# Six weight preparations inside the last block of layer one, in two lanes, and the first pair's ELU values in freed weight tiles

## Chip, core, metric

One core of one Trainium2 chip runs the whole program in one launch. The metric is the device time in microseconds (us), here the median of the runs shown.

## What is computed

Sliding-window attention (window 64, head size 64, 4 batches of 576 positions, 8 heads) gives a 2304 x 512 activation. Two layers follow, each with a 512 x 2048 input matrix and a 2048 x 512 output matrix:

```
x = attention(q, k, v)                      # 2304 x 512, fp32
x = square(relu(x @ moe_w_in)) @ moe_w_out  # layer one
y = elu(x @ moe2_w_in) @ moe2_w_out         # layer two
```

The weights arrive as 64-bit floats and are decoded to fp32 on the chip. Every fp32 operand is split into a high and a low part ("split": ScalarE writes the high part, VectorE the difference), and a product is three matmuls.

## The kernel before

**Layer one** takes the 2304 rows in five blocks (512, 256, 512, 512, 512), `its` in line 424. A block runs 16 iterations j, each a slice of 128 hidden columns. `m_h` (line 354) makes 12 matmuls into a PSUM tile `ph`, of which there are two; ScalarE applies Relu (line 368) and Square (line 369), and the split (line 370) makes `gs`. `m_out` (line 373) multiplies `gs` into four accumulators `o`. The loop issues `m_h` two iterations ahead of `m_out`. TensorE executes in program order, so a late Relu holds the `m_h` two iterations on, which needs its `ph` tile back.

**Layer two** computes its products by a seven-multiplication scheme on 2 x 2 blocks, over three super-blocks b of 768 rows each and eight pairs p of weight slices. `step` (line 578) is one product, six matmuls of 384 columns: numbers 1, 6, 7 and 4 accumulate in one bank `px`, and ScalarE copies `px` to `tmp` after 1, 6 and 7 (line 585); numbers 2, 5 and 3 go to `py` or `po`. `after` (line 602) adds a copy to a bank and applies `elu` (line 563: two ScalarE instructions and one VectorE instruction) into the four values `GR[p]`. The first five products of pair 0 are issued inside the last three iterations of layer one (lines 701 to 703), the rest by the list `seq` (line 721). Then `g_split` and `prod2` multiply the values with the output matrix.

**Operands of layer two** are prepared while layer one runs. `make(i, p)` (line 167) is one of 16 preparations: two loads `praw` of 512 KB, `decode64` of each (one ScalarE and four VectorE instructions), four subtractions or additions (line 184), and seven `put`s. A `put` takes a staging piece `wo` from `small`, splits into it (line 105 on ScalarE, line 106 on VectorE) and stores it to DRAM (`wd1`, `wd2`, 256 KB each). `MAKE` (line 425) names the iterations that issue a `make`; the sixteenth is issued by the `"m"` entry of `seq` at pair 1 (lines 738 and 759). After the attention's pool is closed (the list `la` is filled, line 706) `small` hands out four pieces in a ring (`gs_tile(name, HW, 4)`), and `big` the decode tiles: preparations one and three from then on use the two buffers of tag `y`, the others the old weight tiles `w0` and `w1`.

**Queues.** All transfers are issued by SyncE (SP) in one queue, in program order; an issue whose semaphores are not there yet holds those behind it. `unit_load` (line 473) loads a weight unit `wr` of layer two into a ring of eight tiles, and waits there until TensorE has finished with the ring's old content. ScalarE and VectorE also run in the order that the scheduler wrote.

Of the kernel before, what the change touches and what calls it, by code (L numbers as in the profile page):

```python
# [10 lines left out]
F32 = mybir.dt.float32  # L11
F32R = mybir.dt.float32r
# [4 lines left out]
P = 128  # L17
# [8 lines left out]
def window_attention_then_two_mlps(  # L26
# [395 lines left out]
        return ps_o.tile([P, 512], F32, tag=f"o{rot[0] % KD}", name="po")  # L422

    its = [(t, j) for t in range(NB) for j in range(NJ)]
    MAKE = {(1, 2), (1, 9)} | {(t, j) for t in (2, 3) for j in (1, 5, 9, 13)} | {(4, j) for j in (0, 1, 3, 6, 9)}
    makes = [(i, p) for i in range(2) for p in range(NP)]

    NH = 384
# [8 lines left out]
            return la[0].tile([P, 512], F32, tag="e4", name="ev", bufs=4)  # L437
        return at.tile([P, 512], F32, tag="pt", name="ev", bufs=4)

    turn = [0]  # L440

    def big(shape, name):
        if name == "y" and la:
            turn[0] += 1
        if not la or turn[0] in (1, 3):
            return wts.tile(shape, U32, tag="y", name=name, bufs=2)
        return wts.tile(shape, U32, tag="w0" if name == "y" else "w1", name=name)

    def small(shape, name):
        if la:  # L450
            return gs_tile(name, HW, 4)
        return at.tile(shape, F32R, tag="pt", name=name, bufs=4)

    g_turn = [0]
# [1 line left out]
    def gs_tile(name, n, m):  # L456
        k = g_turn[0] = (g_turn[0] + 1) % m
        if k < 4:
            return la[0].tile([P, 2, n], F32R, tag=f"gs{k}", name=name, bufs=1)
        return wts.tile([P, 2, n], F32R, tag=f"w{LA + NJ - 1}" if k == 4 else f"w{NJ - 1}", name=name)  # L460
# [114 lines left out]
    def add(out, a, b):  # L575
        nc.vector.tensor_tensor(out=out, in0=a, in1=b, op=ALU.add)  # L576

    def step(b, p, i):

        if i == 1:  # L580
            Q[b, p] = {"x": bank(2 if p % 3 == 2 else "x")}
        q = Q[b, p]
        if i in (1, 6, 7):
            prod(b, p, i, q["x"], i == 1, False)
            nc.scalar.activation(out=tmp[i], in_=q["x"][:, :NH], func=AF.Copy)  # L585
        if i == 4:
            prod(b, p, i, q["x"], False, True)
            elu(GR[p][:, 1], q["x"][:, :NH])
        if i == 2:
            q["z"] = bank("a")  # L590
            prod(b, p, i, q["z"], True, True)
        if i == 5:
            q["y"] = bank(1 if p % 2 else "a")
            prod(b, p, i, q["y"], True, False)
        if i == 3:
            prod(b, p, i, q["y"], False, True)
            g = GR[p]
            add(g[:, 2], tmp[6], q["y"][:, :NH])
            elu(g[:, 2], g[:, 2])
            add(g[:, 2], g[:, 2], g[:, 3])  # L600

    def after(b, p, i):
        q, g = Q[b, p], GR[p]
        k, n = (0, "z") if i == 2 else (3, "y")
        add(g[:, k], tmp[1 if i == 2 else 7], q[n][:, :NH])
        elu(g[:, k], g[:, k])

    SRC = {1: 0, 2: 1, 6: 0, 5: 2, 7: 0, 4: 3, 3: 1}
    XY = {}
# [1 line left out]
    def g_split(b, k, p):  # L611
        s = G[b, k, p] = gs_tile("g2", NH, 6)
        g = GR[p]
        split(s[:, 0], s[:, 1], g[:, SRC[k]], nc.vector)
        if k == 1:
            nc.vector.tensor_tensor(out=g[:, 0], in0=g[:, 2], in1=g[:, 0], op=ALU.subtract)
        if k == 2:
            nc.vector.tensor_tensor(out=g[:, 1], in0=g[:, 1], in1=g[:, 0], op=ALU.subtract)
        if k == 6:
            nc.vector.tensor_tensor(out=g[:, 0], in0=g[:, 3], in1=g[:, 0], op=ALU.subtract)  # L620

    G = {}

# [61 lines left out]
    for i, (t, j) in enumerate(its):  # L685
        if i + LA < len(its):
            m_h(*its[i + LA])
        if t + 1 < NB:
            p, r = divmod(j, 3)
            u = (t + 1, p)  # L690
            if p < HP and r == 0:
                load_to(order.index(u) + 1)
                u_S(u, a_alloc)
            elif p < HP and r == 2 and p % 2:
                u_V2([(t + 1, p - 1), u], a_alloc)
        m_out(t, j)
        if t == NB - 1 and j == NJ - 3:
            sy = [wts.tile([P, 2, NH], F32, tag="y", name="sy", bufs=2) for _ in range(2)]
            tmp.update({1: sy[0][:, 0], 6: sy[0][:, 1], 7: sy[1][:, 0]})
            tmp["r"] = [sy[1][:, 1], la[0].tile([P, NH], F32, tag="r", name="r", bufs=1)]  # L700
        if t == NB - 1 and j >= NJ - 3:
            for n in ((1, 2), (6, 5), (7,))[j - NJ + 3]:
                step(0, 0, n)
        if (t, j) == (NB - 2, 3 * HP):
            att.close()
            la.append(pool(ctx, "la", 1))
        if t == 0:
            decode(min(LA + 3 + j, NU))
        elif (t, j) in MAKE:
            make(*makes.pop(0), big, small)  # L710
        elif t == NB - 1 and j == 5:
            x_make(0)
        if t == NB - 1 and j in (8, 10, 12):
            unit_load()
    one.close()
    gb = pool(ctx, "gb", 1, side="right")
    GR += [gb.tile([P, 4, NH], F32, name=f"gr{p}") for p in range(NP)]
    for n, u in ((1, "w0"), (6, "w1"), (7, f"w{LA + NJ - 2}")):
        tmp[-n] = wts.tile([P, MT, HW], F32, tag=u, name="sk")

    seq = []
    Z = NP - 1
    for b in range(NSB):
        def S_(p, *ii, c=b):
            r = []
            for i in ii:
                r += [("s", c, p, i)] + ([("a", c, p, i)] if i in (2, 7) else [])
            return r

        def K_(k, ps=range(NP)):  # L730
            r = []
            for p in ps:
                r += [("k", b, k, p)]
            return r

        for p in range(NP):
            seq.append(("u",))
            if b == 0 and p == 1:
                seq.append(("m",))
            if p == 0:  # L740
                seq += S_(0, 6, 5, 7) if b else [("a", 0, 0, 2), ("a", 0, 0, 7)]
            else:
                seq += S_(p, 1, 2) + S_(p - 1, 3) + S_(p, 6) + S_(p - 1, 4) + S_(p, 5, 7)
        seq.append(("u",))
        seq += K_(1, (0, 1)) + S_(Z, 3, 4) + K_(1, range(2, NP)) + [("u",)] + K_(2) + [("u",)] + K_(6) + [("x", b + 1), ("u",)]
        seq += K_(5) + [("u",)] + K_(7)
        if b + 1 < NSB:
            seq += [("u",)] + S_(0, 1, 2, c=b + 1)
        seq += [("u",)] + K_(4) + [("u",)] + K_(3)
    splits = [s[1:] for s in seq if s[0] == "k"]  # L750
    AHEAD = 3
    for s in seq:
        if s[0] == "s":
            in_turn(step, *s[1:])
        elif s[0] == "a":
            after(*s[1:])
        elif s[0] == "u":
            unit_load()
        elif s[0] == "m":
            with tc.issue_after(last["act"].ins), tc.issue_after(last["dve"].ins):  # L760
                make(*makes.pop(0), big, small)
        elif s[0] == "k":
            g_split(*s[1:])
            in_turn(prod2, *s[1:])
        elif s[1] < NSB:
            x_make(s[1])
# [48 lines left out]
```

## Time and profile before

| | |
|---|---|
| median of 3 runs | 861.9 us (861.79 to 862.55) |
| the profiled execution | 858.92 us, span 857.1 us, granted clock 0.995 |
| TensorE busy (matmul / weight load) | 833.4 us (97%) / 759.2 us (89%) |
| VectorE, ScalarE busy | 598.0 us (70%), 548.3 us (64%) |
| DMA | 185.53 MB, mean 216 GB/s |

The program's last block of layer one lies at about 400 to 490 us of the span, and layer two from there to the end. In a timeline row the columns are start, duration, engine, line, operation, output and input, shape, count; the square bracket behind it is the idle time of the engine ahead of the row and what ended it. A row of a waits view gives the total, the number of waits and the longest.

### The profile page before, as it was taken

To read this page: it belongs to the slowest core of one execution; us is meant where nothing else is said; L and a number is where in the kernel's file an instruction comes from. 1 tells how busy PE (TensorE), PEld (TensorE's weight loads), DVE (VectorE), ACT (ScalarE), POOL (GpSimd) and SP (SyncE) were. 2 spreads that over 40 slices of the span, in tenths; PEclk is the share of its full clock that TensorE was granted. 3 is DMA by queue.
4 is the path that set the end of the run, shared out by engine and by line. 5 is a ranking of instruction groups with operands and counts; after the bars stand their busy time and mean duration, and the time that the engine had idled before them with its cause. 6 is when DMAs were issued, how large, how long until landed. Compare 5 with 4: busy or idle time off the path is not lost.

```text
span 857.1 us, 15143 instructions
## 1 busy us (share of the span) xinstructions
PE 833.4 (97%) x5448; PEld 759.2 (89%) x5448; DVE 598.0 (70%) x1483; ACT 548.3 (64%) x1268; POOL 5.8 (1%) x21
## 2 busy tenths in 40 slices
PE   6899999999999999999999988999999999999997
PEld 5687889998888888888888787999999999999997
DVE  8999978666447574677765677699376787466953
ACT  6787767666456566576654576756477666477552
POOL 2000000000000000000000000000000000000000
PEclk9999999999999999999999999999999999999999
DMA  9991136554145561536578897788777887877831
GB/s 317 363 380 41 40 99 197 192 159 162 52 145 189 189 219 52 170 126 218 212 258 283 285 315 233 294 289 296 239 263 261 320 315 222 282 255 275 286 108 56
DMA packets 78347, 185.53 MB, mean 216 GB/s; under 512 B 24769, under 2 KB 36033, under 8 KB 69825
## 3 DMA queue, kind: packets, MB, share of 16 engines
q1 hardware_dynamic: 78272, 184.57, 63.1%
q8 instruction: 43, 0.70, 0.3%
q14 instruction: 32, 0.25, 0.1%
HBM read 145.75 MB, written 38.80 MB: 215 GB/s over the span
## 4 chain that ended last, share of the span: by engine, by line
PE 82%; DMA 8%; DVE 6%; ACT 2%; issue 1%; SPq 0%; DVEq 0%; ACTq 0%
PE po L634 21%; PE ph L350 19%; PE o L350 18%; PE px L554 7%; PE po L554 5%; PE py L554 5%; DMA wd<-wo 4%; PE pa L268 3%; DMA praw<-in_moe_w_out_dram 3%; PE pa L322 2%; PE pa L309 2%; DMA x2d<-ev 1%; DVE y L146 1%; DVE wo L106 1%; ACT y L135 1%
## 5 line engine op out<-in xcount | busy, mean ns | idle before, releaser
L350 PE MATMUL ph<-xs,w 128*128 128x512 f32 (+1 forms) x960 | 221.2, 373 | 3.7 <-ACT xs L105 2.2
L350 PE MATMUL o<-gs,w 128*128 128x512 f32 (+1 forms) x960 | 216.5, 371 | 0.0
L350 PEld LDWEIGHTS ph<-xs,w 128*128 128x128 f32 x960 | 166.9, 189 | 34.6 <-ACT xs L105 3.1
L350 PEld LDWEIGHTS o<-gs,w 128*128 128x128 f32 x960 | 167.4, 188 | 29.6 <-DVE gs L106 0.2
L634 PE MATMUL po<-wr,g 128*128 128x256 f32 x1512 | 182.9, 283 | 0.3 <-ACT sk L648 0.3
L634 PEld LDWEIGHTS po<-wr,g 128*128 128x128 f32 x1512 | 182.4, 192 | 0.5 <-ACT sk L648 0.5
L105 ACT ACTIVATE g<-gr 128x384 fp32r<-128x384 f32 x168 | 86.7, 522 | 58.9 <-PE po L634 57.9
L106 DVE TENSOR_TENSOR g<-gr,g 128x384 fp32r<-128x384 f32 x168 | 90.9, 555 | 30.3 <-ACT g L105 29.1
L554 PE MATMUL px<-xo,wr 128*128 128x384 f32 x432 | 84.8, 337 | 3.7 <-ACT sy L585 3.6
L105 ACT ACTIVATE wo<-y 128x256 fp32r<-128x256 f32 x112 | 44.4, 412 | 61.4 <-DMA wd<-wo 37.4
L106 DVE TENSOR_TENSOR gs<-g,gs 128x512 fp32r<-128x512 f32 (+1 forms) x80 | 50.7, 634 | 42.7 <-ACT gs L105 41.9
L554 PEld LDWEIGHTS px<-xo,wr 128*128 128x128 f32 x432 | 75.6, 188 | 5.2 <-ACT sy L585 5.0
L106 DVE TENSOR_TENSOR wo<-y,wo 128x256 fp32r<-128x256 f32 x112 | 45.7, 421 | 43.1 <-ACT wo L105 42.2
L368 ACT ACTIVATE g<-ph 128x512 f32<-128x512 f32 (+1 forms) x80 | 43.6, 546 | 39.6 <-PE ph L350 38.4
L136 DVE TENSOR_SCALAR y<-y 128x512 f32<-128x512 f32 (+1 forms) x50 | 24.9, 499 | 53.0 <-ACT y L135 52.8
L554 PE MATMUL py<-xo,wr 128*128 128x384 f32 x288 | 56.8, 336 | 3.3 <-DVE gr L576 3.3
L281 ACT ACTIVATE pb<-pb,nm 128x128 f32<-128x128 f32 x144 | 55.8, 391 | 3.6 <-DVE nm L276 3.3
L554 PE MATMUL po<-xo,wr 128*128 128x384 f32 x288 | 57.3, 339 | 0.2 <-DVE gr L576 0.2
L554 PEld LDWEIGHTS py<-xo,wr 128*128 128x128 f32 x288 | 50.7, 189 | 4.4 <-DVE gr L576 4.2
L554 PEld LDWEIGHTS po<-xo,wr 128*128 128x128 f32 x288 | 51.1, 191 | 0.6 <-DVE gr L576 0.6
L135 ACT ACTIVATE y<-praw 128x512 f32<-128x512 f32 x32 | 21.2, 663 | 44.2 <-DMA praw<-in_moe_w_out_dram 22.1
L585 ACT ACTIVATE sy<-px 128x384 f32<-128x384 f32 x54 | 26.4, 490 | 34.3 <-PE px L554 34.3
(71 smaller groups left out, 945.8 us busy)
## 6 DMA issues: line engine op xcount, KB each, us to landing
wr<-wd SPq DMA_DIRECT2D x66, 1024.0 KB, 6.3
wd<-wo SPq DMA_DIRECT2D x112, 256.0 KB, 3.3
wr<-wd SPq DMA_DIRECT2D x24, 768.0 KB, 4.9
wraw<-in_moe_w_in_dram SPq DMA_DIRECT2D x16, 512.0 KB, 9.6
vr<-in_v_dram SPq DMA_DIRECT2D x16, 512.0 KB, 5.9
wraw<-in_moe_w_out_dram SPq DMA_DIRECT2D x16, 512.0 KB, 9.8
praw<-in_moe_w_in_dram SPq DMA_DIRECT2D x16, 512.0 KB, 3.5
praw<-in_moe_w_out_dram SPq DMA_DIRECT2D x16, 512.0 KB, 3.9
```

Source lines behind the costliest of these rows:

```text
L105: nc.scalar.activation(out=hi, in_=x, func=AF.Copy)
L106: eng.tensor_tensor(out=lo, in0=x, in1=hi.bitcast(F32), op=ALU.subtract)
L135: nc.scalar.activation(out=yf, in_=upper.bitcast(F32), func=AF.Abs)
L136: nc.vector.tensor_scalar(out=yf, in0=yf, scalar1=SHORT, scalar2=TALL, op0=ALU.max, op1=ALU.min)
L268: nc.tensor.matmul(out=ps[:, i * P:(i + 1) * P], lhsT=qr[:, b0 + i].rearrange("p a x -> p (a x)"), rhs=kr[:, o:o + P], start=True, stop=True,)
L281: last["act"] = nc.scalar.activation(out=pb[:, c], in_=pb[:, c], func=AF.Exp, bias=nm[:, b:b + 1], scale=-1.0, accum_out=sm[:, b:b + 1],)
L309: nc.tensor.transpose(out=ps[:, i:i + P], in_=pb[:, i:i + P], identity=ident)
L350: last["pe"] = nc.tensor.matmul(out=ps, lhsT=a[x], rhs=b[y], start=(first and i == 0), stop=(final and i == 2))
L368: nc.scalar.activation(out=g[:, :n], in_=ps[:, :n], func=AF.Relu)
L554: last["pe"] = nc.tensor.matmul(out=ps[:, :NH], lhsT=w[:, wr_, c * P:(c + 1) * P], rhs=x[:, xr_, c], start=first and n == 0, stop=final an ...
L585: nc.scalar.activation(out=tmp[i], in_=q["x"][:, :NH], func=AF.Copy)
L634: last["pe"] = nc.tensor.matmul(out=o, lhsT=s[:, x, m * P:(m + 1) * P], rhs=w[:, y], start=k in (1, 2, 5) and p == 0 and i == 0 and m % 2 ...
```

## The change

`MAKE` issues six preparations in the last block, at j = 0, 1, 3, 4, 6 and 7, in place of five at 0, 1, 3, 6 and 9. The `"m"` entry of `seq` and its branch are gone, and so are the first two `after`s of pair 0 from `seq`: these are now issued right behind products 2 and 7 in the loop, and `m_out` of the iteration is issued behind them. `big` alternates strictly between the tag `y` and `w0`/`w1`. `small` hands out eight pieces, cut from one buffer of each of the four x tags `xs0` to `xs3`, four for odd and four for even preparations. `GR[0]` is taken from `w0` and `w1` inside the loop; two of the output sums (`tmp[-1]`, `tmp[-6]`) take the place that it leaves in pool `gb`.

```diff
-    MAKE = ... | {(4, j) for j in (0, 1, 3, 6, 9)}
+    MAKE = ... | {(4, j) for j in (0, 1, 3, 4, 6, 7)}
...
-    turn = [0]
+    turn = [0, 0]
+    spare = []
...
-        if not la or turn[0] in (1, 3):
+        if not la or turn[0] % 2:
             return wts.tile(shape, U32, tag="y", name=name, bufs=2)
...
     def small(shape, name):
         if la:
-            return gs_tile(name, HW, 4)
+            if not spare:
+                for k in range(KD):
+                    x = xp.tile([P, 2, 2, HW], F32R, tag=f"xs{k}", name=name)
+                    spare.extend((x[:, 0], x[:, 1]))
+            turn[1] += 1
+            return spare[turn[0] % 2 * KD + turn[1] % KD]
...
-        m_out(t, j)
         if t == NB - 1 and j == NJ - 3:
...
+            lo, hi = [wts.tile([P, 2, NH], F32, tag=f"w{i}", name="gr") for i in range(2)]
+            GR.append([lo[:, 0], lo[:, 1], hi[:, 0], hi[:, 1]])
         if t == NB - 1 and j >= NJ - 3:
             for n in ((1, 2), (6, 5), (7,))[j - NJ + 3]:
                 step(0, 0, n)
+                if n in (2, 7):
+                    after(0, 0, n)
+        m_out(t, j)
...
-    GR += [gb.tile([P, 4, NH], F32, name=f"gr{p}") for p in range(NP)]
-    for n, u in ((1, "w0"), (6, "w1"), (7, f"w{LA + NJ - 2}")):
-        tmp[-n] = wts.tile([P, MT, HW], F32, tag=u, name="sk")
+    for p in range(1, NP):
+        g = gb.tile([P, 4, NH], F32, name=f"gr{p}")
+        GR.append([g[:, i] for i in range(4)])
+    for n in (1, 6):
+        tmp[-n] = gb.tile([P, MT, HW], F32, name=f"sk{n}")
+    tmp[-7] = wts.tile([P, MT, HW], F32, tag=f"w{LA + NJ - 2}", name="sk7")
...
-            if b == 0 and p == 1:
-                seq.append(("m",))
             if p == 0:
-                seq += S_(0, 6, 5, 7) if b else [("a", 0, 0, 2), ("a", 0, 0, 7)]
+                seq += S_(0, 6, 5, 7) if b else []
...
-        elif s[0] == "m":
-            with tc.issue_after(last["act"].ins), tc.issue_after(last["dve"].ins):
-                make(*makes.pop(0), big, small)
```

Three places show the new order. First, TensorE at the seam of the layers (`ph` and `o` are layer one, `px` and `py` products of layer two; the last `ph` is that of the last iteration), before:

```order
L350 MATMUL ph<-xs,w 128x512 x12
L350 MATMUL o_4457<-gs,w 128x512 x3
L350 MATMUL o_4458<-gs,w 128x512 x3
L350 MATMUL o_4459<-gs,w 128x512 x3
L350 MATMUL o_4460<-gs,w 128x512 x3
L554 MATMUL px<-xo,wr 128x384 x6
L554 MATMUL py<-xo,wr 128x384 x6
```

and now:

```order
L350 MATMUL ph<-xs,w 128x512 x12
L560 MATMUL px<-xo,wr 128x384 x6
L560 MATMUL py<-xo,wr 128x384 x6
L350 MATMUL o_4454<-gs,w 128x512 x3
L350 MATMUL o_4455<-gs,w 128x512 x3
L350 MATMUL o_4456<-gs,w 128x512 x3
L350 MATMUL o_4457<-gs,w 128x512 x3
```

Products 1 and 2 of pair 0 stand one `m_out` (12 matmuls) earlier.

Second, ScalarE from the last Square of layer one on (`gs` is the split of layer one, `wo` a put, `ev` the eviction of an accumulator, `sy` and `r` temporaries, `gr_5233` the values of pair 0), before:

```order
L369 ACTIVATE g<-g 128x512
L105 ACTIVATE wo<-y 128x256 x2
L105 ACTIVATE gs<-g 128x512
L585 ACTIVATE sy<-px 128x384
L105 ACTIVATE wo<-y 128x256 x3
L585 ACTIVATE sy<-px 128x384
L110 ACTIVATE ev<-o_4457 128x512
L110 ACTIVATE ev<-o_4459 128x512
L567 ACTIVATE sy<-gr_5233 128x384
```

and now (`gr` without a number is pair 0, the ELU lines are 573 and 574):

```order
L369 ACTIVATE g<-g 128x512
L591 ACTIVATE sy<-px 128x384
L105 ACTIVATE gs<-g 128x512
L105 ACTIVATE wo<-y 128x256 x3
L573 ACTIVATE sy<-gr 128x384
L574 ACTIVATE sy<-sy 128x384
L105 ACTIVATE g_5738<-gr 128x384
L591 ACTIVATE sy<-px 128x384
L110 ACTIVATE ev<-o_4454 128x512
L110 ACTIVATE ev<-o_4456 128x512
```

The first ELU of pair 0 stands ahead of the evictions, and the three puts that are left at this point are the last of the program; before, a whole preparation was still to come.

Third, ScalarE in layer two, before, where the sixteenth preparation's puts stood among the copies and ELUs of the first pairs (`gr_5236` and `gr_5237` are pairs 3 and 4):

```order
L567 ACTIVATE r<-gr_5236 128x384
L568 ACTIVATE r<-r 128x384
L567 ACTIVATE sy<-gr_5237 128x384
L568 ACTIVATE sy<-sy 128x384
L105 ACTIVATE wo<-y 128x256
L567 ACTIVATE r<-gr_5236 128x384
L585 ACTIVATE sy<-px 128x384
L105 ACTIVATE wo<-y 128x256
```

and now (`gr_5246` and `gr_5247` are the same pairs):

```order
L573 ACTIVATE r<-gr_5246 128x384
L574 ACTIVATE r<-r 128x384
L573 ACTIVATE sy<-gr_5247 128x384
L574 ACTIVATE sy<-sy 128x384
L573 ACTIVATE r<-gr_5246 128x384
L591 ACTIVATE sy<-px 128x384
```

Nothing stands between them now. From the Relu of the last block's iteration 7 to the end of the block ScalarE has 26 puts in its order, where it had 20.

## Rows read from the trace of the kernel before

**Rows 1.** The page, busy time of the engines, share of the span, instructions.

```profile
PE 833.4 (97%) x5448; PEld 759.2 (89%) x5448; DVE 598.0 (70%) x1483; ACT 548.3 (64%) x1268; POOL 5.8 (1%) x21
```

**Rows 2.** Windows: stretch, length, busy of PE, PEld, DVE, ACT, POOL, clock, DMA share, GB/s.

```profile
430.00:487.00 57.00, 55.43 (x249) 45.96 (x248) 34.57 (x71) 28.88 (x58) 0.00 (x0) 1.00 0.81 276
...
487.00:535.00 48.00, 41.25 (x216) 38.42 (x215) 33.85 (x73) 31.74 (x72) 0.00 (x0) 0.96 0.82 278
620.00:680.00 60.00, 60.00 (x367) 60.00 (x366) 41.25 (x81) 44.27 (x95) 0.00 (x0) 1.00 0.77 279
```

**Rows 3.** Timeline of PE around the seam, the rows with idle time and two without.

```profile
473.72 3.01 PE L350 MATMUL ph<-xs,w 128*128 128x512 f32 x12 [1.08 <-ACT g L368]
...
485.69 1.31 PE L554 MATMUL px<-xo,wr 128*128 128x384 f32 x6 [0.49 <-ACT sy L585]
...
492.87 1.31 PE L554 MATMUL py<-xo,wr 128*128 128x384 f32 x6 [0.41 <-DVE gr L576]
495.74 1.31 PE L554 MATMUL py<-xo,wr 128*128 128x384 f32 x6 [1.56 <-DVE gr L576]
...
511.89 1.31 PE L554 MATMUL py<-xo,wr 128*128 128x384 f32 x6 [1.31 <-DVE gr L576]
...
520.02 1.33 PE L554 MATMUL po<-xo,wr 128*128 128x384 f32 x6 [0.24 <-DVE gr L576]
...
527.56 1.79 PE L554 MATMUL px<-xo,wr 128*128 128x384 f32 x6 [3.07 <-ACT sy L585]
...
533.41 1.20 PE L554 MATMUL po<-xo,wr 128*128 128x384 f32 x6
534.45 1.20 PE L554 MATMUL px<-xo,wr 128*128 128x384 f32 x6
```

**Rows 4.** Windows of the same columns, behind the longest stall.

```profile
527.56:531.06 3.50, 3.50 (x12) 3.50 (x13) 3.19 (x7) 2.77 (x7) 0.00 (x0) 0.59 0.85 202
531.06:534.00 2.94, 2.94 (x17) 2.87 (x17) 2.09 (x5) 1.81 (x4) 0.00 (x0) 0.91 1.00 411
```

**Rows 5.** Timeline of ACT at the seam and in layer two.

```profile
489.65 0.42 ACT L105 ACTIVATE wo<-y 128x256 fp32r<-128x256 f32 x1 [2.87 <-DMA wd<-wo]
...
493.28 0.47 ACT L585 ACTIVATE sy<-px 128x384 f32<-128x384 f32 x1
...
509.37 0.67 ACT L135 ACTIVATE y<-praw 128x512 f32<-128x512 f32 x1 [2.10 <-DMA praw<-in_moe_w_out_dram]
...
526.30 0.42 ACT L105 ACTIVATE wo<-y 128x256 fp32r<-128x256 f32 x1 [4.24 <-DMA wd<-wo]
```

**Rows 6.** Groups of instructions, 490 to 535 us: count, busy, mean ns, idle before.

```profile
L106 DVE TENSOR_TENSOR wo<-y,wo 128x256 fp32r<-128x256 f32 x9 | 3.7, 423 | 7.8 <-ACT wo L105 7.8
L105 ACT ACTIVATE wo<-y 128x256 fp32r<-128x256 f32 x9 | 3.6, 413 | 7.3 <-DMA wd<-wo 7.3
...
L143 DVE SCALAR_TENSOR_TENSOR y<-praw,y 128x512 uint32<-128x512 uint32 x2 | 1.4, 690 | 0.0
...
L135 ACT ACTIVATE y<-praw 128x512 f32<-128x512 f32 x2 | 1.3, 657 | 2.1 <-DMA praw<-in_moe_w_out_dram 2.1
```

**Rows 7.** Timeline of PE and of ACT in the last block, iteration 13.

```profile
461.60 2.88 PE L350 MATMUL ph<-xs,w 128*128 128x512 f32 x12
...
471.12 0.90 ACT L105 ACTIVATE wo<-y 128x256 fp32r<-128x256 f32 x2 [4.55 <-DMA wd<-wo]
...
473.07 0.59 ACT L368 ACTIVATE g<-ph 128x512 f32<-128x512 f32 x1
```

**Rows 8.** Waits of ACT, 437 to 487 us: total, times, longest.

```profile
ACT wo L105 <- DMA wd<-wo: 11.0, 3, 4.6
ACT y L135 <- DMA praw<-in_moe_w_out_dram: 6.6, 3, 3.0
```

**Rows 9.** Stores of puts, count, size, median us to landing: 430 to 487, 487 to 535.

```profile
wd<-wo SPq DMA_DIRECT2D x21, 256.0 KB, 4.8
...
wd<-wo SPq DMA_DIRECT2D x10, 256.0 KB, 6.5
```

More of the change, by code (lines that the diff above doesn't have):

```diff
@@ L424, in window_attention_then_two_mlps @@
     its = [(t, j) for t in range(NB) for j in range(NJ)]
-    MAKE = {(1, 2), (1, 9)} | {(t, j) for t in (2, 3) for j in (1, 5, 9, 13)} | {(4, j) for j in (0, 1, 3, 6, 9)}
+    MAKE = {(1, 2), (1, 9)} | {(t, j) for t in (2, 3) for j in (1, 5, 9, 13)} | {(4, j) for j in (0, 1, 3, 4, 6, 7)}
     makes = [(i, p) for i in range(2) for p in range(NP)]
@@ L587, in step @@
             prod(b, p, i, q["x"], False, True)
-            elu(GR[p][:, 1], q["x"][:, :NH])
+            elu(GR[p][1], q["x"][:, :NH])
         if i == 2:
@@ L597, in step @@
             g = GR[p]
-            add(g[:, 2], tmp[6], q["y"][:, :NH])
-            elu(g[:, 2], g[:, 2])
-            add(g[:, 2], g[:, 2], g[:, 3])
+            add(g[2], tmp[6], q["y"][:, :NH])
+            elu(g[2], g[2])
+            add(g[2], g[2], g[3])
     def after(b, p, i):
@@ L604, in after @@
         k, n = (0, "z") if i == 2 else (3, "y")
-        add(g[:, k], tmp[1 if i == 2 else 7], q[n][:, :NH])
-        elu(g[:, k], g[:, k])
+        add(g[k], tmp[1 if i == 2 else 7], q[n][:, :NH])
+        elu(g[k], g[k])
     SRC = {1: 0, 2: 1, 6: 0, 5: 2, 7: 0, 4: 3, 3: 1}
@@ L613, in g_split @@
         g = GR[p]
-        split(s[:, 0], s[:, 1], g[:, SRC[k]], nc.vector)
+        split(s[:, 0], s[:, 1], g[SRC[k]], nc.vector)
         if k == 1:
-            nc.vector.tensor_tensor(out=g[:, 0], in0=g[:, 2], in1=g[:, 0], op=ALU.subtract)
+            nc.vector.tensor_tensor(out=g[0], in0=g[2], in1=g[0], op=ALU.subtract)
         if k == 2:
-            nc.vector.tensor_tensor(out=g[:, 1], in0=g[:, 1], in1=g[:, 0], op=ALU.subtract)
+            nc.vector.tensor_tensor(out=g[1], in0=g[1], in1=g[0], op=ALU.subtract)
         if k == 6:
-            nc.vector.tensor_tensor(out=g[:, 0], in0=g[:, 3], in1=g[:, 0], op=ALU.subtract)
+            nc.vector.tensor_tensor(out=g[0], in0=g[3], in1=g[0], op=ALU.subtract)
     G = {}
@@ L714, in window_attention_then_two_mlps @@
             unit_load()
+    assert not makes
     one.close()
     gb = pool(ctx, "gb", 1, side="right")
-    GR += [gb.tile([P, 4, NH], F32, name=f"gr{p}") for p in range(NP)]
-    for n, u in ((1, "w0"), (6, "w1"), (7, f"w{LA + NJ - 2}")):
-        tmp[-n] = wts.tile([P, MT, HW], F32, tag=u, name="sk")
+    for p in range(1, NP):
[4 more added lines that the diff above has]
+    tmp[-7] = wts.tile([P, MT, HW], F32, tag=f"w{LA + NJ - 2}", name="sk7")
     seq = []
```

## The prediction

> **What bounds the kernel now.** First the page: TensorE is busy for 833.4 of 857.1 us [rows 1], so all its idle time together is some 24 us, and the question is how much of that lies where the change acts. Next the windows [rows 2]. In the last block TensorE misses 1.57 us of 57 (430 to 487), in layer two's first pairs 6.75 us of 48 (487 to 535, with a granted clock of 0.96), and in the second super-block, which runs the same products with no preparation beside it, none of 60. So the place to read is the seam. The timeline of TensorE [rows 3] gives each stall there and who ended it: in the last block 1.08 (the Relu of iteration 13 was late) and 0.49; in layer two 0.41, 1.56, 1.31, 0.24 and 3.07, all ended by VectorE's `gr` additions or ScalarE's `sy` copies. Last, what kept those two engines. ScalarE stood still in layer two until a store of a put had landed (2.87 and 4.24 us) and until a load of the sixteenth preparation had (2.10) [rows 5]. Since it runs in order, the copies and ELUs that TensorE wants stood behind these. The 3.07 us stall of TensorE ended at 527.56, when ScalarE was free at 526.30 and had made the copy; the 2.87 us wait belongs to the fifteenth preparation, whose last three puts stand in front of the first copies of layer two.
>
> **What the stalls of layer two cost.** Idle: 0.41 + 1.56 + 1.31 + 0.24 + 3.07 = 6.59 us. Clock: in the two stretches behind the 3.07 us gap the granted clock is 0.59 and 0.91 [rows 4], the lower of its two levels (1.2 GHz) for most of the first stretch, after TensorE had stood still. In numbers: from 527.56 to 533.41 TensorE did 24 matmuls, four groups of six; a group at full clock takes 534.45 - 533.41 = 1.04 us [rows 3], so 4.16 us became 5.85, a loss of 1.69. The gaps of 1.56 and 1.31 show no such loss. Together 8.28 us.
>
> **What the change removes there.** One preparation leaves: on ScalarE two decodes of 0.66 and seven puts of 0.41, 4.2 us; on VectorE eight decode instructions of at most 0.69, seven puts and four subtractions of 0.42, at most 10.1 us [rows 6]; on SP's queue two loads and seven stores. With them go the waits of 2.10 and 4.24 us and so the stalls of 1.31, 0.24 and 3.07 with the clock behind the last: 4.62 + 1.69 = 6.31 us. What covers the rest of these pairs is shown by the second super-block: the same products, copies and ELUs, and TensorE loses nothing in 60 us [rows 2].
>
> The stalls of 0.41 and 1.56 are another matter: they are product 2 of pair 1 and product 3 of pair 0, which wait for the two `after` additions of pair 0. Product 3 needs product 7's copy (0.47) and an addition (0.55), 1.0 us of work, while TensorE has the two products of pair 1 ahead, 2.1 us. It waited since the copies of product 7 and of pair 1 only ran from 493.28 on [rows 5], behind the 2.87 us wait, two evictions and the first ELU. In the new order product 2 stands one `m_out` earlier, its addition and ELU stand ahead of the evictions, and what remains in front is three puts. I keep 0.4 us of the 1.97, since the three puts can still wait for stores; bounds 0 (the 2.1 us of cover hold) and 1.97 (nothing gained).
>
> **What it adds in the last block.** ScalarE's 4.2 us and VectorE's 10.1 us cost nothing by themselves: from 430 to 487 they are busy 28.88 and 34.57 us of 57 [rows 2], and what fills the rest are waits. Moved in front of the loop's end, the addition and ELU of `GR[0]` (three instructions of some 0.5 us, twice) fit there too. The waits are what counts. ScalarE lost 11.0 us to stores and 6.6 us to loads between 437 and 487, 17.6 us [rows 8], in a stretch in which its order has 20 puts. TensorE has slack for that: the Relu of iteration 13 came at 473.07, after its `ph` was done at 464.48, and that lateness of 8.6 us cost 1.08 us [rows 7, 3]. So about 7.5 us of lateness is free, and what comes on top is paid.
>
> Now 26 puts stand where 20 stood, six sevenths of a preparation more. Two things work against each other. More transfers: 6/7 of 2.88 MB on 15.7 MB (276 GB/s for 57 us), 18.2 MB or 319 GB/s in the same stretch; that is more than the busiest long stretches show (278 and 279) [rows 2]. But fewer reasons to wait: the last three preparations before shared four pieces and one pair of decode tiles, so each put waited for the store four puts back, whichever preparation it was from, and a first load waited until the preparation before had left its tile. Now two preparations own four pieces and a decode pair each, the next first load can go out early, and while ScalarE waits for one lane the other's transfers run on. Lower bound: both stalls of the last block go, -1.57. Upper bound: the waits grow with the puts, 17.6 x 6/20 = +5.3 us, all of it paid since the slack is used up, and one fall of the clock as above, +1.69: +7.0. I take +1.0, nearer the lower end, because ScalarE's waits of before are mostly the ring's (11.0 of 17.6), and since only the part above 7.5 us of lateness at one iteration is paid.
>
> SP's queue: the stores and loads stand in front of the weight units of pairs 1 to 4 and hold those for as long as they wait. Units 0 to 3 fill the ring of eight tiles; the next can't start before TensorE frees one, so a delay of some us there is covered. The moved output sums and the `GR` of other pairs sit in places that are free when they are first written, behind the block's end; nothing.
>
> **Sum.** -6.59 - 1.69 + 0.4 + 1.0 = -6.9 us. The profiled execution goes from 858.9 to 852.0. The median of the runs lies 3.0 us above that execution, and the same step from 861.9 gives **855.0 us**.
>
> The Trainium skill speaks against packing more transfers into one block: "DMA: Bandwidth & Descriptors", section Specifications, gives a core about 358 GB/s of HBM. By that figure, an estimate, 18.2 MB need 51 us of the block's 57, and if nine tenths were too full, the time would be that of the second rival, 869.1. The window at 531 us moved 411 GB/s [rows 4], so a short burst passes the figure here; no run here shows how long that can last.
>
> **Rivals.**
> 1. *The waits just grow.* The block takes the upper bound: -8.28 + 0.4 + 7.0 = -0.9, **861.0**. For it: the lateness at iteration 13 is at the edge already, so each further us is paid. Against: the lanes. Chance 0.15.
> 2. *The last block becomes bound by its transfers*, and the kernel slower. Place: ScalarE's puts and `praw` decodes between iterations 7 and 15. Price: with a fuller queue a store takes not 4.8 us to land but 6.5, as between 487 and 535 [rows 9], so the waits are 17.6 x 26/20 x 6.5/4.8 = 31.0, 13.4 us more; -8.28 + 0.4 + 13.4 + 1.69 = +7.2, **869.1**. It decides from the point where lateness exceeds the free 7.5 us by more than the 8.3 us saved. Against: ScalarE overlaps the waits of two lanes, and loads that are issued earlier are waited for less. Chance 0.07.
> 3. *The first `after`s do not get earlier in fact.* The three last puts wait for their stores as the fifteenth preparation's did (2.87), and the 1.97 us stay while the rest goes: -6.31 + 1.0 = -5.3, **856.6**. Chance 0.18.
> 4. *Both stalls of the block go as well*: -8.28 - 1.57 = -9.9, **852.0**. Chance 0.15.
>
> The forecast has 0.45.
>
> **How the numbers follow.** The cases in order are 852.0, 855.0, 856.6, 861.0 and 869.1. The range 851.0 to 861.5 takes in all but the last with some 0.5 us on each side for the runs' spread, and what of the first rival lies above 861.5 is left out: about 0.1 in all with the second. Two parts in a thousand, 1.7 us, is about what a measurement of this kernel can tell from no change. Faster by more than that means under 860.2: the forecast, rivals 3 and 4 and a fifth of rival 1, 0.81. Within it: the most of rival 1, 0.11. Slower: the second and a little of the first, 0.08.
>
> **What the profile after will show.** Right: no put and no `praw` decode on ScalarE behind about 490 us; TensorE without idle above 0.5 us from pair 1 on, the clock at 1.00 throughout 490 to 550, and layer two's first `prod2` some 6 us nearer to the end of layer one. In the last block idle of TensorE below 3 us, ended by ScalarE's Relu, and a DMA rate above 300 GB/s between 430 and 487. Wrong: several waits of 4 us and more for `wd` or `praw` stacked on ScalarE between two Relus, TensorE's `ph` waiting for `g`, or the granted clock down before 487. If 0.41 and 1.56 are still there, it is the three puts. The second half of the program (from 570 us on) should be the same row for row; any change of time there would be none of my steps.

## The result, and the profile after

The changed kernel takes **847.85 us** (median of 4 runs, 847.81 to 849.41), beside 861.85 us of the kernel before (4 runs, 860.52 to 862.55): ratio 0.9844, 95% interval 0.9827 to 0.9861. It is 14.0 us faster, twice the 6.9 us that were forecast, and lies below the range. Between the two profiled executions the gain is 9.5 us (858.92 and 849.41).

The page of the changed kernel, span and busy time, beside [rows 1]:

```profile
span 847.6 us, 15130 instructions
...
PE 831.8 (98%) x5448; PEld 760.3 (90%) x5448; DVE 596.7 (70%) x1483; ACT 548.8 (65%) x1268; POOL 6.3 (1%) x21
```

The engines do the same work. Windows of the changed kernel, columns as in [rows 2]:

```profile
430.00:487.00 57.00, 57.00 (x259) 47.83 (x258) 42.62 (x93) 35.33 (x72) 0.00 (x0) 1.00 0.93 332
487.00:535.00 48.00, 48.00 (x276) 47.73 (x275) 31.99 (x62) 34.83 (x76) 0.00 (x0) 1.00 0.67 245
620.00:680.00 60.00, 60.00 (x391) 60.00 (x390) 44.73 (x89) 42.44 (x91) 0.00 (x0) 1.00 0.77 277
```

TensorE is busy for all of 57 us in the last block (55.43 before) and for all of 48 us behind it (41.25 before), at full clock throughout. The DMA engines' load has moved with the preparation: 0.93 in the block, where it was 0.81, and 0.67 behind it, where it was 0.82.

The timeline of TensorE, changed kernel, answers [rows 3]. The first row is the last `ph`, then products 1 and 2 of pair 0, then the rows of the next products, now without idle time, then the first output product and the two rows behind it with idle time:

```profile
473.37 2.88 PE L350 MATMUL ph<-xs,w 128*128 128x512 f32 x12
476.09 1.23 PE L560 MATMUL px<-xo,wr 128*128 128x384 f32 x6
477.15 1.20 PE L560 MATMUL py<-xo,wr 128*128 128x384 f32 x6
...
490.66 2.24 PE L560 MATMUL py<-xo,wr 128*128 128x384 f32 x12
492.74 2.24 PE L560 MATMUL px<-xo,wr 128*128 128x384 f32 x12
...
540.58 2.31 PE L640 MATMUL po<-wr,g 128*128 128x256 f32 x18
...
578.01 3.76 PE L640 MATMUL po<-wr,g 128*128 128x256 f32 x27 [0.17 <-DVE g L106]
582.89 5.18 PE L640 MATMUL po<-wr,g 128*128 128x256 f32 x41 [1.13 <-DVE g L106]
```

All seven stalls of [rows 3] are gone. The two idle times at 578 and 583 us are new in this execution; the experiment `h_change_again` comes back to them.

What ScalarE waited for in the last block, changed kernel, 430 to 487 us (before, 437 to 487: [rows 8]):

```profile
ACT wo L105 <- DMA wd<-wo: 7.0, 7, 1.8
ACT wo L105 <- DVE y L146: 5.1, 5, 2.4
ACT y L135 <- DMA praw<-in_moe_w_out_dram: 2.7, 2, 2.1
ACT wo L105 <- DVE y L184: 2.1, 3, 1.1
```

And how long the transfers of the block took to land, changed kernel, 430 to 487 us:

```profile
wd<-wo SPq DMA_DIRECT2D x31, 256.0 KB, 6.5
...
praw<-in_moe_w_out_dram SPq DMA_DIRECT2D x5, 512.0 KB, 5.7
```

These two views have to be read together. A store takes longer to land than before (6.5 us, 4.8 in [rows 9]), there are more of them (31, not 21), and yet ScalarE waits 9.7 us for transfers where it waited 17.6, no single time longer than 2.1 us.

How late ScalarE came to the Relu tells the same. In the prediction's iteration 13, changed kernel (the `ph`, then its Relu):

```profile
462.49 2.88 PE L350 MATMUL ph<-xs,w 128*128 128x512 f32 x12
```

```profile
467.39 0.58 ACT L368 ACTIVATE g<-ph 128x512 f32<-128x512 f32 x1
```

The Relu started 2.0 us after its `ph` was done (465.37), where it was 8.6 us late before [rows 7]. From iteration 7 to the end of the block the largest lateness is 4.0 us.

A measure that the experiments use: the time from the start of iteration 13's `ph` to the first product with the output matrix ("the stretch"). Before it is 461.60 to 552.13, **90.53 us**; after 462.49 to 540.58, **78.09 us**. Both stretches hold the same 421 matmuls. With no stall in it, 78.09 is what TensorE's work there takes.

### The profile page after: what moved, and what is told of

It reads as the page before. It is cut to its first block, busy times and chain, and to the rows that moved or that the text cites. A ratio compares the mean times of both kernels' runs of the same rounds, so it can differ in the third digit from the quotient of the medians.

```text
span 847.6 us, 15130 instructions
## 1 busy us (share of the span) xinstructions
PE 831.8 (98%) x5448; PEld 760.3 (90%) x5448; DVE 596.7 (70%) x1483; ACT 548.8 (65%) x1268; POOL 6.3 (1%) x21
## 4 chain that ended last, share of the span: by engine, by line
PE 94%; DVE 2%; DMA 2%; ACT 1%; issue 0%; SPq 0%; DVEq 0%; ACTq 0%
PE ph L350 24%; PE o L350 23%; PE po L640 19%; PE px L560 9%; PE py L560 6%; PE po L560 6%; PE pa L268 3%; PE pa L322 2%; PE pa L309 2%; DMA out_dram<-ev 1%; DMA xq<-x2d 1%; DVE pb L276 1%; DVE pb L297 1%; PE po L268 0%; DMA wraw<-in_moe_w_in_dram 0%; ACT pb L281 0%
## 5 line engine op out<-in xcount | busy, mean ns | idle before, releaser
L582 DVE TENSOR_TENSOR gr<-sy,py 128x384 f32<-128x384 f32 x48 | 26.6, 554 | 31.9 <-PE py L560 20.5
```

## Experiments

Every ratio is to the kernel before on the same chip, with its 95% interval.

**The kernel before again** (no edit).

> The kernel before, once more, to see how much its own executions differ. Its timed runs lay 3.0 us above its profiled execution, and the change gained 14.0 us in the timed runs and 9.5 us between the two profiled executions. Theory: the waits for stores and loads on ScalarE fall differently in each execution, so the stretch from the last block's iteration 13 to the first product with the output matrix (90.5 us in the profile of before, 78.1 us after) differs by some us between executions of the same kernel; a second profile shows a stretch of 91 to 95 us, and the median is 861 to 862.5. Rival: that stretch is the same within 0.5 us and the 3 us lie elsewhere (the start, or layer two's later part).

Measured: 859.62 us (10 runs, 858.24 to 863.52), ratio 0.999 (0.9969 to 1.0012). Its profile, timeline of TensorE, two of the stalls and the first output product:

```profile
511.92 1.34 PE L554 MATMUL py<-xo,wr 128*128 128x384 f32 x6 [1.79 <-DVE gr L576]
...
526.78 1.73 PE L554 MATMUL px<-xo,wr 128*128 128x384 f32 x6 [2.29 <-ACT sy L585]
...
551.36 2.31 PE L634 MATMUL po<-wr,g 128*128 128x256 f32 x18
```

The same stalls with other sizes (1.31 and 3.07 in [rows 3]); the stretch is 90.91 us. So the two profiled executions agree within 0.4 us, as the rival had it: the stretch of 91 to 95 did not show, and the median lies under the 861 us expected. But both are at the lower end of what this kernel does: over all comparisons its 52 timed runs go from 856.4 to 865.5 us, and the profiled ones are 858.9 and 858.2 (nine of the 52 are below 858.92). The mean clock of the runs goes along, but loosely: six runs with 1.000 average 859.1 us, eight runs with 0.993 or less 862.1, five with 0.994 863.4 and five with 0.997 858.3. How the 3 us are spread over the slower executions, no profile shows.

**Lanes alone.** Edit, on the kernel before (the sixteenth preparation keeps the old ring and tiles, the others get two lanes):

```diff
-        if not la or turn[0] in (1, 3):
+        if not la or turn[0] in (1, 3, 5):
...
-        if la:
+        if la and turn[0] == NP - 1:
             return gs_tile(name, HW, 4)
+        if la:
+            if not spare:
...
+            return spare[turn[0] % 2 * KD + turn[1] % KD]
```

> Only the two lanes: odd and even preparations of the last block own four staging pieces and a pair of decode tiles each; five preparations in the block at the old places, the sixteenth still in layer two on the old ring, the first values of layer two as before. Theory: ScalarE's waits of 17.6 us in the last block fall to about half, the two stalls there (1.08 and 0.49) go, the 0.41 and 1.56 at the seam shrink, and the 1.31, 0.24, 3.07 with the clock behind them stay: 857 to 859 us. Rival, lanes matter only for the sixth preparation: within 1 us of the kernel before.

Measured: 854.6 us, ratio 0.9913 (0.9882 to 0.9944), 2.4 us better than the forecast's near edge. Timeline of TensorE, the rows with idle time:

```profile
491.95 1.33 PE L562 MATMUL py<-xo,wr 128*128 128x384 f32 x6 [1.11 <-DVE gr L584]
...
509.22 1.31 PE L562 MATMUL py<-xo,wr 128*128 128x384 f32 x6 [2.42 <-DVE gr L584]
...
521.74 1.32 PE L562 MATMUL px<-xo,wr 128*128 128x384 f32 x6 [0.80 <-ACT sy L593]
...
525.88 1.31 PE L562 MATMUL py<-xo,wr 128*128 128x384 f32 x6 [0.72 <-DVE gr L584]
```

No stall in the block, 1.11 us instead of 0.41 and 1.56 behind it, and the sixteenth preparation costs less than before although its own ring and tiles are the old ones: its longest stall is 2.42 us, and the clock stays up (1.00 from 487 to 535). Stretch 84.52. Not as expected: ScalarE's waits in the block did not fall to half; those for stores are still 11.3 us and those for loads 5.4 (430 to 487). But no Relu of the block comes more than 6.1 us late (8.6 before), and TensorE doesn't pay.

**The change with the old seam.** Edit, on the change: the values of pair 0 in pool `gb`, the two `after`s in `seq`, `m_out` ahead of the products.

```diff
-                if n in (2, 7):
-                    after(0, 0, n)
...
-                seq += S_(0, 6, 5, 7) if b else []
+                seq += S_(0, 6, 5, 7) if b else [("a", 0, 0, 2), ("a", 0, 0, 7)]
```

> The change without its seam part: six preparations in two lanes, but the values of pair 0 in the late pool, their first two additions and ELUs issued in layer two, and m_out ahead of the products as before. Theory by the rows of before: product 2 of pair 1 and product 3 of pair 0 wait again for these additions, 2.8 us from start to start, so 847.9 + 2.8 = 850.7 us. Rival: those waits came from the fifteenth preparation's last puts, which no longer stand there with a landing wait of 2.9 us, and the result is within 1 us of the change, 847 to 849.

Measured: 848.22 us, ratio 0.9845 (0.9816 to 0.9874). Timeline of TensorE, the one stall left, and the first output product:

```profile
492.35 1.31 PE L560 MATMUL py<-xo,wr 128*128 128x384 f32 x6 [1.11 <-DVE gr L582]
...
541.34 2.31 PE L640 MATMUL po<-wr,g 128*128 128x256 f32 x18
```

The stretch is 79.46 us: the seam part is worth 1.37 us in the profile, half of the 2.8 expected, and the ratio can't be told from the change's 0.9844. So each side has half of it. The time is the rival's, but one stall of 1.11 us is left where 0.41 and 1.56 were: 0.86 of the 1.97 us went with the fifteenth preparation's last puts, and the 1.11 are the old seam's.

**The change with one ring of four pieces.**

```diff
         if la:
-            if not spare:
...
-            return spare[turn[0] % 2 * KD + turn[1] % KD]
+            return gs_tile(name, HW, 4)
```

> The change with the staging pieces taken back to one ring of four for both lanes; six preparations in the block, decode tiles in two lanes, early values of pair 0. Theory: the ring is what made ScalarE wait, so its waits for stores in the last block are 14 us or more again (7.0 after, 14.1 before), TensorE waits for Relu or for gs there, 852 to 858 us. Rival: the decode lanes alone do it, 847 to 849.

Measured: 851.5 us (848.34 to 854.68), ratio 0.9877 (0.9838 to 0.9917); stretch 85.35. ScalarE's largest wait in the block (430 to 487), and the two larger stalls of TensorE:

```profile
ACT wo L105 <- DMA wd<-wo: 15.3, 7, 4.5
```

```profile
491.74 1.32 PE L555 MATMUL px<-xo,wr 128*128 128x384 f32 x6 [2.40 <-ACT sy L586]
494.23 2.29 PE L555 MATMUL py<-xo,wr 128*128 128x384 f32 x6 [1.17 <-DVE gr L577]
```

The theory holds for the waits for stores (14 or more expected); the time sits just below its range, and the place is another. TensorE waits for no Relu and no `gs` in the block, which loses 0.3 us only: the lateness is paid behind it, at the first copies, which stand among the last puts (the last one starts at 489.32, in the change at 481.52).

**The move alone.** Edit, on the kernel before: the six iterations of the change, no `"m"` entry; one ring, decode tiles and seam as before.

```diff
-    MAKE = {(1, 2), (1, 9)} | {(t, j) for t in (2, 3) for j in (1, 5, 9, 13)} | {(4, j) for j in (0, 1, 3, 6, 9)}
+    MAKE = {(1, 2), (1, 9)} | {(t, j) for t in (2, 3) for j in (1, 5, 9, 13)} | {(4, j) for j in (0, 1, 3, 4, 6, 7)}
...
-            if b == 0 and p == 1:
-                seq.append(("m",))
```

> Only the sixth preparation moved into the last block (at the change's iterations 0, 1, 3, 4, 6, 7); one ring of four staging pieces, decode tiles as before (the last four preparations share one pair), seam as before. Theory: without lanes each of ScalarE's waits comes on top of the other, 6 us more of them in and behind the block; of the stalls of layer two only those of the sixteenth preparation go. By the stretch from iteration 13 to the first output product (90.9 us before, 85.4 with one ring and two decode lanes, 78.1 with all), 84 to 89 us; 852 to 858 us in all. Rival: moving is the larger part and lanes are only worth what they are with a sixteenth preparation in layer two, 848 to 850 us.

Measured: **864.65 us**, ratio 1.0058 (1.0037 to 1.0079), slower than before and beyond both expectations; stretch 95.3. Timeline of TensorE, four of its six stalls, and a window behind the longest:

```profile
475.35 3.02 PE L350 MATMUL ph<-xs,w 128*128 128x512 f32 x12 [1.81 <-ACT g L368]
488.43 1.31 PE L554 MATMUL px<-xo,wr 128*128 128x384 f32 x6 [1.59 <-ACT sy L585]
...
500.00 2.29 PE L554 MATMUL py<-xo,wr 128*128 128x384 f32 x6 [3.71 <-DVE gr L576]
...
523.34 1.34 PE L554 MATMUL py<-xo,wr 128*128 128x384 f32 x6 [2.77 <-DVE gr L576]
```

```profile
504.00:508.00 4.00, 4.00 (x14) 4.00 (x13) 3.40 (x7) 1.51 (x4) 0.00 (x0) 0.50 0.10 35
```

The sixth preparation does not end in the block: its last loads and puts stand among layer two's first copies. Its second load is issued, and its last put starts, at

```profile
496.99 0.33 SPq L172 DMA_DIRECT2D praw<-in_moe_w_out_dram  x1
```

```profile
520.59 0.41 ACT L105 ACTIVATE wo<-y 128x256 fp32r<-128x256 f32 x1
```

In the block TensorE loses 1.81 + 1.59 us (1.57 before), behind it 8.83 us (6.59 before). ScalarE's waits for transfers in the block are 19.8 us, hardly more than the 17.6 of before.

**Two rings, decode tiles as before**, with the new seam:

```diff
-        if not la or turn[0] % 2:
+        if not la or turn[0] in (1, 3):
```

> The change with its eight pieces in two lanes, but the decode tiles as before (only preparations one and three in tag y, the last four one after the other in the tiles w0 and w1, which the values of pair 0 then wait for). Theory: the first load of each late preparation waits for the one before to leave its tiles, so ScalarE's waits for loads grow from 2.7 us in the block to 6 or more and the last preparation ends some us later, in front of the first copies of layer two: 850 to 854 us. Rival: the staging ring alone made the waits, within 1 us of the change, 847 to 849.

Measured: 868.83 us, ratio 1.0106 (1.0077 to 1.0135); stretch 97.62. Timeline of TensorE:

```profile
509.45 3.88 PE L560 MATMUL py<-xo,wr 128*128 128x384 f32 x12 [12.38 <-DVE gr L582]
```

The waits for loads grow as expected (7.8 us in the block). The values of pair 0 lie in the tiles that the last preparation decodes into, and the addition that ends the wait of 12.38 us starts on VectorE right behind the last put there (508.84, the put's instruction 508.38). The direction is as expected; the price is 21 us over the change where 2 to 6 were forecast. The last of the experiments shows that the shared tile isn't the reason: without it the addition stands at the same place.

**Later places**, with all else as in the change:

```diff
-    MAKE = {(1, 2), (1, 9)} | {(t, j) for t in (2, 3) for j in (1, 5, 9, 13)} | {(4, j) for j in (0, 1, 3, 4, 6, 7)}
+    MAKE = {(1, 2), (1, 9)} | {(t, j) for t in (2, 3) for j in (1, 5, 9, 13)} | {(4, j) for j in (0, 1, 3, 6, 9, 11)}
```

> The change with its six preparations at iterations 0, 1, 3, 6, 9 and 11 instead of 0, 1, 3, 4, 6 and 7: lanes and seam as in the change. Theory: with lanes the place matters by when the last put is done; at iteration 11 the last preparation has some 25 us left and ends behind the block, in front of the first copies: 849 to 853 us. Rival: the scheduler's order decides and the later places only spread the transfers, 847.5 to 848.5 us.

Measured: 846.8 us, ratio 0.9851 (0.9824 to 0.9879); stretch 78.09. The rival was right: between these two choices the iterations named in `MAKE` make no difference. The edit did not make the last put late, though: ScalarE starts it at 481.64, in the change at 481.52. So this experiment doesn't test what a late last put costs.

**The change again** (no edit).

> The change once more. Its profiled execution lost 1.3 us in layer two's output products, waiting for a g split behind a late load of xq, and took 307.0 us from the first output product to the end where all other kernels take 305.0. Theory: that is one execution's accident, most executions lie within 0.5 us of 847.8 and the stretch is 78.1 us again. Rival: the change causes it, and the profile shows the stall again at the same place.

Measured: 846.79 us (846.53 to 847.55), ratio 0.9849 (0.9817 to 0.9882); the chip is another one, and the kernel before is quicker on it too (860.1). The stretch is 78.09 again and the rest of the span 305.5 us, where the first profile had 307.0 and every other kernel 305.0 to 305.5. The new stalls at 578 and 583 us belong to that one execution: 0.2 us is left of 1.3.

Four more kernels complete the table of the three parts: decode lanes, second ring, move.

**Decode lanes alone**, on the kernel before:

```diff
-        if not la or turn[0] in (1, 3):
+        if not la or turn[0] in (1, 3, 5):
```

> The kernel before with only the decode tiles in two lanes (five preparations in the block, the sixteenth in layer two, one ring of four pieces, old seam). Both lanes together gained 6.6 us here. Theory now: the decode lane is the larger part, since it lets a preparation's first load and decode run while the one before still puts; 855 to 857 us. Rival: the pieces' ring is what ScalarE stands at (11 us of waits for stores), and without the second ring the gain is under 2 us, 859 to 861.

Measured: 857.02 us, ratio 0.9949 (0.993 to 0.9967), at the upper edge of the theory's range. Its reason shows in part: ScalarE's waits for loads in the block fall (4.5 us, 6.6 before), but those for stores rise (14.9, 11.0 before), and TensorE loses no less there (1.17 and 0.78 us) than before. The gain lies behind the block, where the fifteenth preparation's last put starts at 484.82 and not at 490.28.

**Second ring alone**, on the kernel before: the pieces of "lanes alone" without its first edit.

> The kernel before with only the second ring of pieces (decode tiles as before, the sixteenth in layer two, old seam). Theory now: with one decode pair there is seldom a second preparation to use the other ring, so it stays within 2 us of before, 858 to 862. Rival: the ring is the larger part, 855 to 857.

Measured: 864.09 us, ratio 1.0044 (1.0028 to 1.0059), slower than before; neither expected it to harm. ScalarE's waits in the block, 430 to 487 us:

```profile
ACT wo L105 <- DVE y L146: 9.9, 6, 2.4
ACT y L135 <- DMA praw<-in_moe_w_out_dram: 7.8, 3, 3.2
ACT wo L105 <- DMA wd<-wo: 6.7, 3, 3.9
```

Waits for stores fell (before, over the same 57 us, 11.0), but those for VectorE's decode (6.0 before) and for loads (6.6) grew by as much: the first puts stand closer behind the decode in ScalarE's order, and ScalarE waits there. TensorE's longest stall is 5.31 us, at the first copy of layer two. The cause is its place in ScalarE's order, here behind the fifteenth preparation's last two puts:

```profile
488.67 0.42 ACT L105 ACTIVATE wo<-y 128x256 fp32r<-128x256 f32 x1 [4.14 <-DMA wd<-wo]
489.33 0.42 ACT L105 ACTIVATE wo<-y 128x256 fp32r<-128x256 f32 x1 [0.24 <-DMA wd<-wo]
489.65 0.47 ACT L593 ACTIVATE sy<-px 128x384 f32<-128x384 f32 x1
```

and in the kernel before ahead of the last three:

```profile
485.17 0.47 ACT L585 ACTIVATE sy<-px 128x384 f32<-128x384 f32 x1
```

**Move with decode lanes, one ring, old seam**: "the change with the old seam" with `small` as in "one ring".

> Six preparations in the block with decode tiles in two lanes, one ring of pieces, old seam. With the new seam the same took 851.5. Theory: decode lanes make the move pay (849 to 853 us, where no lanes took 864.7), the second ring is worth 2 to 4 us more. Rival: it was the early values that held it down, and with the old seam it is 855 or more.

Measured: 852.98 us, ratio 0.9908 (0.9884 to 0.9932), in the theory's range; the second ring is worth 4.8 us beside "the change with the old seam" (848.22), more than the 2 to 4 expected. The sixth preparation's last load is issued, and its last put starts, much earlier than in "the move alone":

```profile
476.55 1.41 SPq L172 DMA_DIRECT2D praw<-in_moe_w_out_dram  x1
```

```profile
493.45 0.42 ACT L105 ACTIVATE wo<-y 128x256 fp32r<-128x256 f32 x1 [0.38 <-DMA wd<-wo]
```

**Move with two rings, old decode tiles, old seam**: the same kernel with the second ring and `turn[0] in (1, 3)`.

> Six preparations in the block with two rings of pieces, decode tiles as before (the last four share one pair), old seam, so that no value of layer two waits for a decode tile. With the new seam the same took 868.8, of which 12.4 us were one wait for those tiles. Theory: one decode pair serialises the last four preparations whatever the seam, and the last one ends in layer two: 860 to 866 us. Rival: only the shared tile made it slow, and with the old seam it comes to 849 to 853.

Measured: 868.33 us, ratio 1.0087 (1.0063 to 1.011). The theory's direction holds, 2.3 us above its range; the shared tile with pair 0's values was not the reason. VectorE starts the first additions of pair 0 at 508.77, again right behind the last put (its instruction there at 508.43), and TensorE waits 5.88 and 7.36 us.

All eight with the old seam together, as ratios to the kernel before:

| | one ring | two rings |
|---|---|---|
| sixteenth in layer two, one decode pair late | 1 (before) | 1.0044 |
| sixteenth in layer two, decode lanes | 0.9949 | 0.9913 |
| six in the block, one decode pair late | 1.0058 | 1.0087 |
| six in the block, decode lanes | 0.9908 | 0.9845 |

Each row without decode lanes loses by the second ring and by the move; each row with them gains by both. The loss by the ring alone and its gain in the last row are clear of the intervals; its effect in the two middle rows (0.9949 to 0.9913, 1.0058 to 1.0087) is not. The move's effect is clear of them in three of the four pairs; with one ring and decode lanes (0.9949 to 0.9908) the intervals just touch.

## Why the prediction was wrong

**What held.** The stalls of layer two were read rightly: ScalarE's in-order waits for the sixteenth preparation's transfers and the fifteenth's last puts held the copies that TensorE wanted. In the change the 1.31, 0.24 and 3.07 us and the fall of the clock are gone. The signs named for the profile are there: no put starting behind 481.52 us, full clock from 487 to 535, over 300 GB/s in the block (332). The first output product comes 11.55 us earlier, where some 6 were named. The free lateness of some 7.5 us held as well: in the profiled kernels the stalls of `ph` that a Relu ended (0.62 to 1.81 us) all follow a Relu that was 8.1 us late or more, and where no Relu of iterations 7 to 14 was later than 6.2 us there is none.

**The step that failed is the last block's term**, +1.0 us with bounds -1.57 and +7.0. It took ScalarE's waits as growing with the number of puts (17.6 x 6/20), and with them a lateness that was at its limit already. In the change ScalarE waited 9.7 us and not more than 17.6, its lateness at iteration 13 was 2.0 us and not 8.6, and the block lost nothing: -1.57. The lanes were named there and as a reason against both rivals, but given too little weight, and the ring was taken for the main thing (11.0 of 17.6). The experiments show that the decode lanes decide the sign: the move costs 0.4 to 0.6% without them and gains 0.4 to 0.7% with them, and the ring alone harms. With a pair of tiles for each of two preparations the next loads go out earlier: the block's last load is issued at 496.99 us in the move alone, at 476.55 with decode lanes, and at 464.65 in the change.

**The place of the price was wrong too.** The term prices lateness inside the block. In the kernels with six preparations there, most of it is paid behind the block, where the copies of layer two stand among the last puts. By the start of the last put on ScalarE they fall into three groups: up to 482 us (the change, its repeat, the later places, the old seam) the stretch is 78.09 to 79.46 us; at 489 and 493 (one ring, new and old seam) 85.35 and 85.57; from 508 on (one decode pair late) 95.3 to 100.0. The sum of ScalarE's waits in the block does not order them: it is 20.7 us in the move with decode lanes and one ring (852.98 us), and 14.5 with the second ring alone (864.09), where the kernel before has 17.6. The 864.65 us of the move alone lie between rival 1 and rival 2 (861.0 and 869.1), but neither has its place right. That the last put's time is itself the cause, and not only goes along with it, is read from the stalls that end there; no run moved it alone.

**What the 7.1 us between forecast and result consist of.** The block's term gives 2.57 us, the seam's residue 0.4, the price of the stalls 2.59 and the base 1.55; the next paragraphs take them in turn. With the block's term at its lower bound and no residue the same sum is rival 4's 852.0, so the median fell below the range by the last two.

**Rival 2's premise held and its conclusion did not.** Stores took 6.5 us to land, the very figure it used, and ScalarE waited less. A landing time is paid only where an engine stands at that transfer; with one ring the same six preparations wait 15.3 us for stores, with two 7.0, and the landing takes 6.6 and 6.5 us. The rate that the Trainium skill's page "DMA: Bandwidth & Descriptors", section Specifications, gives as a core's share of HBM, about 358 GB/s, was approached and not reached as a mean over the block (332 GB/s over 57 us, DMA share 0.93), with no idle time of TensorE. No run here shows a stretch of that length beyond it.

**The price of a stall was too low.** I added idle times from the timeline: 6.59 + 1.57 + 1.69 for the clock = 9.85 us. The stretch became 12.44 us shorter. The difference is in how the idle column is made: it runs from the modelled end of a matmul to the next start. Take three rows of the kernel before, timeline of TensorE:

```profile
489.78 2.68 PE L554 MATMUL px<-xo,wr 128*128 128x384 f32 x12
...
509.37 1.21 PE L554 MATMUL py<-xo,wr 128*128 128x384 f32 x6
...
552.13 2.31 PE L634 MATMUL po<-wr,g 128*128 128x256 f32 x18
```

A group of six takes 1.04 us from start to start, so what follows the first row was due at 491.86 and started at 492.87: 1.01 us lost, where the row ahead of the start says 0.41 (0.44 lie inside the row of twelve, 2.68 us long where it takes 2.24 elsewhere). Behind the second it was due at 510.41 and came at 511.89: 1.48 for 1.31. Over the seven stalls the losses from start to start are 1.25, 0.67, 1.01, 1.83, 1.48, 0.40 and 3.24, 9.88 us instead of 8.16. With the clock's 1.69 that is 11.57; the last 0.9 is spread over rows that come 0.1 to 0.2 us late without an idle entry, most of them the first behind a stall.

**The base was one execution.** The 14.0 us between the medians are the 9.5 between the profiles, plus 2.9 by which the median of before lay above its profile, plus 1.6 by which the change's profile lay above its median. The 9.5 are the stretch's 12.44, less 2.05 in the output products (1.5 of it the accident that the repeat does not have) and 0.89 by which iteration 13 began later. I carried a step measured in one fast execution of before over to a median 3.0 us above it, unchanged. That kernel's stalls hang on when transfers land (they differ by up to 0.9 us between its two profiles), so its slower executions may have had more to give; no profile of one shows it.

**The seam's residue** of 0.4 us is 0. The seam part itself is worth 1.37 us in the profile and no measurable time; of the 1.97 us of idle time it took 1.11, and 0.86 went with the fifteenth preparation's waits. So rival 3 had part of the cause for those stalls, and the puts that it feared no longer wait long: the last three start at 480.24 to 481.52, behind waits of 1.79, 0.23 and 0.22 us.

## What to carry to other kernels

Before moving transfer-bound work to where an in-order engine has spare time, give consecutive pieces of it separate buffers at every stage: here the move cost 0.4 to 0.6% without a second pair of decode tiles and gained 0.4 to 0.7% with one, while a second ring of staging pieces alone made things worse. Ask what stands behind the last piece of the moved work in the engine's order, and not only how long the engine waits in all. Price a stall from start to start against the same instructions where they run undisturbed, not from the idle column. And where a kernel's own executions scatter by 9 us, ask what part of the scatter the change takes away.

## What the runs showed of the hardware that I had not expected

The kernel before scatters from 856.4 to 865.5 us over 52 runs; the change, with the same work and the same transfers, from 846.5 to 849.4 over 8. I read it so: once TensorE waits for no engine that waits for a transfer, the spread of landing times leaves the total almost alone. No run tests this by itself. The stores' landing time rose by a third (4.8 to 6.5 us), and TensorE lost nothing in that block. The clock fell to its lower level behind some stalls and not behind others, and the stall's length alone does not tell which: in the kernel before run again the granted clock behind 2.29 us is 0.50 (528.5 to 530.5), while it is 1.00 behind 2.42 us in "lanes alone" and behind 2.77 us in the move alone (523.34 to 526). The windows of the first two:

```profile
528.50:530.50 2.00, 2.00 (x8) 2.00 (x7) 2.00 (x6) 1.08 (x4) 0.00 (x0) 0.50 0.64 215
```

```profile
509.22:511.50 2.28, 2.28 (x13) 2.28 (x14) 2.28 (x5) 2.22 (x5) 0.00 (x0) 1.00 0.11 47
```

Where it fell it cost 1.69 us in the kernel before, and in the move alone, where it is 0.50 from 504 to 508 us, 2.45 us (18 matmuls of 384 columns from 503.40 to 508.97, 3.12 us at full clock).
